# A long convolution with gating on one core: the second stage's early loads cut in halves and issued by ScalarE

## The chip, the cores and the metric

The kernel runs on 1 core of one Trainium2 chip. The metric is the device time of one execution in microseconds (us). The core has five engines that work side by side: TensorE (PE; its weight loads are PEld), VectorE (DVE), ScalarE (ACT), GpSimd (POOL) and SyncE (SP). Sixteen DMA engines move data between the chip's memory and SBUF. All data are f32.

## The reference, cut to what matters

Eight sequences of 6400 rows and 128 channels are convolved along the rows with a filter that is as long as a sequence. The result goes through a gated product: a causal convolution of five taps per channel with a sigmoid, times a projection, and a second projection.

```python
Xf = np.fft.rfft(x, n=2 * S, axis=1)          # x: 8 x 6400 x 128
Hf = np.fft.rfft(h, n=2 * S, axis=0)          # h: 6400 x 128
y = np.fft.irfft(Xf * Hf[None], n=2 * S, axis=1)[:, :S]
...
for k in range(5):
    gate_pre += conv_w[k] * yp[:, k:k + S, :] # yp: y behind four rows of zeros
gate = 1.0 / (1.0 + np.exp(-gate_pre))
out = (gate * (y @ w_val)) @ w_out
```

## The kernel before, in words

The transform of 6400 points is split into 100 x 64 and made of matmuls. A sequence passes four stages.

1. First stage (`Forward`): sums and differences of x (`sums`, on POOL) and products with the table `r1` (`half`), written to `gy`. Its input comes in 16 pieces `x_81` to `x_83`, three buffers of 256 KB; `sums` also issues the load of the piece three places ahead.
2. Second stage (`s2_mm`, `Product`): 13 blocks. Block kb multiplies `gy` with block kb of the table `m2` (512 KB), multiplies the result on DVE with block kb of the filter's spectrum (`hd` in the chip's memory, 512 KB, loaded into `h_sb`), and adds on POOL back into `gy`. `m2` has three buffers and the spectrum four; all seven are parts of one tile, `ring`. A block's buffer is loaded anew when its block is done (`m2_load(kb + M2B)`, `h_load(kb + HB)`).
3. Third stage (`s3_quads`): 16 groups over `gy`. Per group TensorE makes the products with `r3`; ScalarE copies one half of the result to a part of `ring` (`keep`, 128x512) and two edges to `dt` (`ends`); DVE joins both halves into `dt` (two joins).
4. Fourth stage (`Chunk`): 13 chunks over `dt`, with the table `m4` in `m4_sb`, then the taps, the sigmoid, both projections and the store to `out`.

The stages of neighbouring sequences are interlaced. The loop over the 16 groups `g` of the third stage of sequence b also holds one `half` and one `sums` of the first stage of sequence b + 1 and the remaining taps and projections of sequence b - 1 (`steps[g]`). The loop behind it holds the fourth stage of b and the second stage of b + 1. A "third stage" below means the first of these loops with all that is in it. In the first sequence there is no earlier one, and its loop also forms the weights `w_sb` (`wgen`) and loads pieces of `m4` (`m4_load`, of five rows of the table each) in the order of the list `m4_rest`.

The order on every engine is that of the program: `_Engines` wraps each engine so that instructions stay in the order written. The profile therefore names line 112, the wrapper's, for all of them, and groups are told apart by their tiles (`pt` is PSUM; `r_sb`, `m_sb` and `sd` are the tables and the sums). SyncE issues every DMA, also in program order: an issue whose buffer isn't free keeps the later ones waiting. Of the second stage's blocks, `m2` 0 to 2 and spectrum 0 to 2 are loaded ahead, in the third stage's loop, at the groups that the table `AHEAD` gives: `AHEAD[g] = (1, kb)` is spectrum block kb, `(0, kb)` is table block kb. Spectrum block 3 uses the buffer that `keep` writes, so it is loaded behind the last group.

Parts of `ring` also hold outputs and taps of the sequence before (`held_c`, `held_y`, `keeps`). So a load ahead has to wait until the chunk that uses its place has been stored. A landing is told by one of eight counters, which the DMAs of the program take in turn.

Of the kernel before, what the change touches and what calls it, by code (L numbers as in the profile page):

```python
# [16 lines left out]
C = 128  # L17
# [7 lines left out]
SB = 4  # L25
# [5 lines left out]
CH = 5  # L31
# [8 lines left out]
M2B = 3  # L40
MH = 6
HB = 4
XB = 3
XH = 8
AHEAD = {2: (1, 0), 7: (0, 0), 9: (0, 1), 10: (0, 2), 11: (1, 1), 13: (1, 2)}


def _out_range(ch):
# [76 lines left out]
def longconv_moe(ctx: ExitStack, tc: tile.TileContext, x, h, r1, m2, r3, m4, w64, out):  # L125
    nc = _Engines(tc)
# [24 lines left out]
    m2_sb = [r.rearrange("p (s a c) -> p s a c", a=2, c=C) for r in ring_at[:M2B]]  # L151
    h_sb = [ring_at[M2B + i] for i in (2, 0, 1, 3)]
# [9 lines left out]
    hd = dp.tile([NKB, 128, 2 * SB * C], F32, name="hd")  # L162
# [68 lines left out]
    def single():  # L231
        return ps1.tile([128, 512], F32, name="pt1", tag="pt1")
# [47 lines left out]
    def count(kb):  # L280
        return min(SB, HR - kb * SB)
# [7 lines left out]
    def m2_load(kb, ms=m2_sb):  # L289
        if kb < NKB:  # L290
            n = count(kb)
            nc.sync.dma_start(ms[kb % len(ms)][:, :n], m2[:, kb * SB : kb * SB + n])

    def h_load(kb):
        if kb < NKB:
            n = 2 * count(kb) * C
            nc.sync.dma_start(h_sb[kb % HB][:, :n], hd[kb, :, :n])

    def laid(t, kb):
        n = count(kb)  # L300
        return t[:, : 2 * n * C].rearrange("p (c d k t) -> p c d k t", c=2, k=n, t=2)
# [54 lines left out]
    def s3_quads(d0):  # L356
        pt = pair()
        for q in range(4):
            for c in range(2):
                for r, k in ((0, 0), (1, 0), (1, 1), (0, 1)):  # L360
                    d, o = k * HP + d0 + q, (r + k) % 2
                    w = d // 2 * 2 * N1 + c * 2 * HR + d % 2
                    v = pt[o * HP : (o + 1) * HP, k, q * 2 * N2 : (q + 1) * 2 * N2].rearrange("p (b m) -> p b m", b=2)
                    nc.tensor.matmul(
                        v[:, :, c::2],
                        lhsT=gyf[r * HP : (r + 1) * HP, w : w + 2 * HP - 1 : 2],
                        rhs=r3_sb[r * HP : (r + 1) * HP, c, :],
                        start=True,
                        stop=True,
                    )  # L370
        v = pt.rearrange("p k (d b m) -> p b m k d", b=2, m=N2)
        a = d0 // 4 % 2 * 512
        t = h_sb[HB - 1][:, a : a + 512]
        o = dv.rearrange("p n c (k d) -> p (n c) k d", k=2)[:, :, :, d0 : d0 + 4]

        def keep():
            act(
                t.rearrange("p (m c d) -> p m c d", c=2, d=2 * XG)[:, :, ::-1],
                pt.rearrange("p k (d b m c) -> p b m c (k d)", b=2, m=N2 // 2, c=2)[:, 1],
            )  # L380

        def join(op, n):
            u = t.rearrange("p (m k d) -> p m k d", k=2, d=XG)
            nc.vector.tensor_tensor(out=n, in0=v[:, 0, 2:], in1=u[:, 2:], op=op)

        def ends():
            act(o[:, 0:2], v[:, 0, :2])
            act(o[:, N2 : N2 + 2], v[:, 1, :2])

        return keep, ends, lambda: join(ADD, o[:, 2:N2]), lambda: join(ALU.subtract, o[:, : N2 + 1 : -1])  # L390
# [171 lines left out]
        m2_load(kb, m2_head)  # L562
    nc.sync.dma_start(r3_sb, r3)

    def m4_load(j):
        a = slice(CH * j, CH * j + CH + (j == 12))
        nc.sync.dma_start(m4_sb[:, a], m4.rearrange("k (n t) -> k n t", t=MW)[:, a])

    m4_rest = [12, 7, 5, 8, 4, 9, 10, 11, 6]
    sp, pr = {0: Spectrum(0)}, {}  # L570
    for kb in range(-1, NKB + 1):
        if 0 <= kb < NKB:
            pr[kb] = Product(kb, sp[kb].h, t_head[kb % 3], m2_head)
            m2_load(kb + MH, m2_head)
        if kb + 2 < NKB:
            sp[kb + 2] = Spectrum(kb + 2)
        if kb + 1 < NKB:
            sp[kb + 1].copy()
            sp[kb + 1].store()
        if 0 <= kb < NKB:  # L580
            pr[kb].mul_u()
            pr[kb].mul_t()
            pr[kb].add(nc.vector if kb == NKB - 1 else nc.gpsimd)
        if 0 <= kb < M4H:
            m4_load(kb)
# [10 lines left out]
    for b in range(B):  # L596
        nxt = b + 1 < B


        steps = collections.defaultdict(list)  # L600
        for c in pend:
            a = c.ch[0]
            if a == HEAD[0]:
                t = NS - 1
            elif c.held:
                t = (a - HELD) // CH
            else:
                k = (a - WAIT) // CH
                t = max(3 + k, 2 + 2 * k)
                steps[2 * k] += [lambda c=c: c.taps(range(2))]  # L610
                steps[2 * k + 1] += [lambda c=c: c.taps(range(2, 4)), c.add]
            steps[t] += [c.project, c.sigm, c.gate]
            if t + 2 < NS:
                steps[t + 2] += [c.output]
                steps[t + 3] += [c.store]
        pend = [c for c in pend if c.ch[0] in (HEAD[0], HEAD[0] - CH)]
        for g in range(NS):
            e = s3_quads(4 * g)
            f = []
            if nxt:  # L620
                f = fx.half([single(), single()])
                fx.sums(nc.gpsimd)
            for u in e:
                u()
            for u in f:
                u(act)
            if b == 0:
                next(wgen, None)
                next(wgen, None)
                if g % 3 == 0 and g < 12:  # L630
                    m4_load(m4_rest.pop(0))
            if nxt and g in AHEAD:
                f, kb = AHEAD[g]
                (h_load if f else m2_load)(kb)
            for u in steps[g]:
                u()
        if nxt:
            h_load(HB - 1)
        if b + 2 < B:
            fx = Forward(x[b + 2], gy)  # L640


        chs = CHUNKS if not nxt else sorted(CHUNKS, key=lambda c: (c != HEAD, c[0] > 0, c[0] < LATE))
        cs = [Chunk(b, i, ch, nxt) for i, ch in enumerate(chs)]
        jobs = collections.defaultdict(list)
        for i, c in enumerate(cs):
            if i and not c.late and not c.held:
                jobs[i + 3].append(c)
        if not nxt:
            jobs[NCH + 2].append(cs[0])  # L650
        pr = {}

        def s2(kb):
            if nxt and kb < NKB:
                pr[kb] = Product(kb)
                m2_load(kb + M2B)

        def times(kb):
            if kb in pr:
                pr[kb].mul_u()  # L660
                pr[kb].mul_t()
                pr.pop(kb).add()
                h_load(kb + HB)

        outs, at = [], 0
        for s in range(max(NCH, *jobs) + 2):
            kbs = list(range(at, min(at + 2 - s % 2, NKB))) if nxt else []
            at += len(kbs)
            if s == 0:
                s2(0)  # L670
            if s < 2:
                cs[s].s4()
            late = pend[s : s + 1]
            if late and s == 0:
                late[0].output()
                late[0].store(p_t[1][:, : HEAD[1]])
                late = []
            for kb in kbs[:1]:
                s2(kb + 1)
            if m4_rest:  # L680
                m4_load(m4_rest.pop(0))
            for c in jobs[s]:
                c.project()
            if 1 < s < NCH:
                cs[s].s4()
            for c in outs + late:
                c.output()
            for c in jobs[s]:
                c.sigm()
            for kb in kbs[:1]:  # L690
                times(kb)
            for kb in kbs[1:]:
                s2(kb + 1)
            if s < NCH:
                cs[s].copies()
            for c in outs + late:
                c.store()
            for kb in kbs[1:]:
                times(kb)
            if 0 < s <= NCH and not cs[s - 1].late:  # L700
                cs[s - 1].taps()
            if 2 < s < NCH + 2 and not cs[s - 2].late:
                cs[s - 2].add()
            for c in jobs[s]:
                c.gate()
            outs = jobs[s]
            if b + 2 < B:
                if s == 5:
                    fx.load(XB)
                if s in (9, 10):  # L710
                    fx.sums(nc.gpsimd)
        pend = [cs[0]] + [c for c in cs if c.held or c.late]
# [45 lines left out]
```

## Time and profile before

| | us |
|---|---|
| median of 3 runs | 983.11 |
| lowest, highest | 981.2, 993.21 |
| the profiled execution | 983.02 |
| its span in the trace | 980.9 |

The span runs from the first to the last instruction; the execution is 2.1 us longer. In the trace the eight third stages begin at about 99, 207, 319, 430, 543, 655, 765 and 877 us, and the fourth stage that follows each takes the rest to the next. Each line of a view names an engine, an operation, what it writes and reads (out<-in), the shape and how often (x); behind it stand the time, and in brackets the engine's idle time ahead of it and what ended that. "issue" as a releaser means that the profile shows nothing the engine waited for.

### The profile page before, as it was taken

To read this page: it belongs to the slowest core of one execution; us is meant where nothing else is said; L and a number is where in the kernel's file an instruction comes from. 1 tells how busy PE (TensorE), PEld (TensorE's weight loads), DVE (VectorE), ACT (ScalarE), POOL (GpSimd) and SP (SyncE) were. 2 spreads that over 40 slices of the span, in tenths; PEclk is the share of its full clock that TensorE was granted. 3 is DMA by queue.
4 is the path that set the end of the run, shared out by engine and by line. 5 is a ranking of instruction groups with operands and counts; after the bars stand their busy time and mean duration, and the time that the engine had idled before them with its cause. 6 is when DMAs were issued, how large, how long until landed. Compare 5 with 4: busy or idle time off the path is not lost.

```text
span 980.9 us, 47924 instructions
## 1 busy us (share of the span) xinstructions
PE 861.9 (88%) x21360; PEld 695.4 (71%) x21360; DVE 749.7 (76%) x1049; ACT 507.6 (52%) x1215; POOL 574.1 (59%) x594
## 2 busy tenths in 40 slices
PE   7799759988899989998899989989799988998797
PEld 6698758965688557965688557976588657874564
DVE  5547647878788788878797887878888786878686
ACT  4422443277624774177624774168624775156476
POOL 5447644866377664867367654866458664852132
PEclk9899789999999999999999999999999999999999
DMA  7776456826494465926495375834485365911112
GB/s 252 242 271 235 156 184 222 310 57 206 139 320 144 130 218 176 317 57 175 141 309 174 110 224 163 316 95 160 157 293 190 110 206 161 324 33 55 53 43 104
DMA packets 76365, 177.41 MB, mean 181 GB/s; under 512 B 17792, under 2 KB 29312, under 8 KB 76160
## 3 DMA queue, kind: packets, MB, share of 16 engines
q1 hardware_dynamic: 76160, 174.35, 53.8%
q8 instruction: 168, 2.75, 1.2%
q14 instruction: 37, 0.30, 0.1%
HBM read 141.56 MB, written 32.77 MB: 178 GB/s over the span
## 4 chain that ended last, share of the span: by engine, by line
PE 52%; DVE 13%; issue 8%; ACT 5%; DMA 4%; POOL 1%; SPq 0%; DVEq 0%; ACTq 0%; POOLq 0%
PE pt L112 52%; DVE ring L112 6%; DVE dt L112 4%; DMA ring<-m 3%; ACT ring L112 3%; DVE gl L112 2%; DVE gy L112 1%; POOL gl L112 1%; ACT gy L112 1%; ACT dt L112 1%; DMA out<-dt 0%; ACT p L112 0%; ACT yl L112 0%; POOL ring L112 0%; ACT gl L112 0%
## 5 line engine op out<-in xcount | busy, mean ns | idle before, releaser
L112 POOL TENSOR_TENSOR gy<-gy,ring 128x512 f32<-128x512 f32 (+1 forms) x182 | 220.3, 1242 | 119.0 <-ACT p L112 51.1
L112 PEld LDWEIGHTS pt<-r_sb,gy 64*64 64x64 f32 x8192 | 149.4, 140 | 107.8 <-issue 68.5
L112 DVE TENSOR_TENSOR dt<-pt,ring 128x496 f32<-128x496 f32 x256 | 160.0, 666 | 82.1 <-ACT dt L112 49.5
L112 PEld LDWEIGHTS pt<-m_sb,dt 128*64 128x64 f32 x4096 | 186.4, 136 | 30.3 <-issue 12.1
L112 POOL TENSOR_TENSOR sd<-x 128x256 f32<-128x256 f32 x236 | 185.4, 815 | 31.4 <-issue 19.7
L112 PE MATMUL pt<-r_sb,gy 64*64 64x64 f32 x8192 | 166.7, 228 | 41.6 <-issue 30.3
L112 PE MATMUL pt<-m_sb,dt 128*64 128x100 f32 x4096 | 194.4, 249 | 8.8 <-DVE ring L112 6.4
L112 PE MATMUL pt<-gy,ring 128*64 128x128 f32 x3008 | 188.2, 278 | 11.9 <-DMA ring<-m 5.2
L112 ACT COPY ring<-pt 128x512 f32<-128x512 f32 (+2 forms) x216 | 129.0, 603 | 130.8 <-PE pt L112 79.4
L112 PEld LDWEIGHTS pt<-gy,ring 128*64 128x64 f32 x3008 | 174.7, 135 | 24.5 <-PE pt L112 9.9
L112 PE MATMUL pt<-r_sb,sd 50*64 50x100 f32 x4608 | 148.0, 263 | 30.4 <-issue 20.9
L112 DVE TENSOR_TENSOR gy<-pt,ring 128x1024 f32<-128x1024 f32 (+1 forms) x99 | 117.0, 1181 | 59.3 <-PE pt L112 57.5
L112 PEld LDWEIGHTS pt<-r_sb,sd 50*64 50x64 f32 x4608 | 123.7, 144 | 37.9 <-issue 26.7
L112 DVE TENSOR_TENSOR ring<-pt,ring 128x1024 f32<-128x1024 f32 (+2 forms) x131 | 134.4, 1026 | 6.7 <-ACT ring L112 0.2
L112 ACT COPY gy<-pt 128x400 f32<-128x400 f32 x248 | 111.4, 506 | 34.2 <-PE pt L112 33.3
L112 ACT COPY yl<-pt 128x500 f32<-128x500 f32 (+1 forms) x89 | 51.1, 574 | 132.0 <-PE pt L112 125.4
L112 POOL TENSOR_TENSOR gl<-gl,p 128x500 f32<-128x500 f32 (+1 forms) x45 | 53.2, 1184 | 110.8 <-DVE gl L112 89.2
L112 ACT COPY dt<-pt 128x16 f32<-128x16 f32 (+3 forms) x317 | 67.2, 264 | 91.2 <-PE pt L112 91.0
L112 DVE SCALAR_TENSOR_TENSOR gl<-yl,w_sb,gl 128x500 f32<-128x500 f32 (+1 forms) x112 | 99.5, 893 | 2.1
L112 PE MATMUL pt<-ring,w_sb 128*64 128x500 f32 x320 | 80.1, 598 | 8.9 <-DVE ring L112 8.8
L112 DVE SCALAR_TENSOR_TENSOR ring<-pt,w_sb,ring 128x500 f32<-128x500 f32 (+3 forms) x94 | 63.1, 671 | 6.1 <-ACT ring L112 1.5
L112 POOL TENSOR_TENSOR ring<-ring,p 128x500 f32<-128x500 f32 (+1 forms) x23 | 24.7, 1074 | 60.7 <-DVE ring L112 44.1
(58 smaller groups left out, 781.0 us busy)
## 6 DMA issues: line engine op xcount, KB each, us to landing
ring<-m SPq DMA_DIRECT2D x90, 512.0 KB, 5.3
ring<-hd SPq DMA_DIRECT2D x84, 512.0 KB, 5.1
x<-xl SPq DMA_DIRECT2D x118, 256.0 KB, 3.0
out<-ring SPq DMA_DIRECT2D x40, 250.0 KB, 3.4
out<-yl SPq DMA_DIRECT2D x40, 250.0 KB, 2.8
m_sb<-m SPq DMA_DIRECT2D x12, 375.0 KB, 5.7
hd<-ring SPq DMA_DIRECT2D x8, 512.0 KB, 4.5
out<-dt SPq DMA_DIRECT2D x16, 250.0 KB, 4.4
```

What stands on the lines that cost most here:

```text
L112: return self._tc.keep_in_program_order(call(*args, **kwargs))
```

## The change

`AHEAD` has twelve entries in place of six. Each loads one half of a block (256 KB): of a spectrum block the first or second half of its columns, of a table block the first or second two of its four slices. They stand at groups 0, 1 and 6 to 15, one a group. ScalarE issues them, and the place in the loop is another: behind `keep`, `ends` and the joins of the group, ahead of the copies of the first stage, where before it was behind those copies. In the first sequence, the four `m4` pieces of the loop (at groups 0, 3, 6 and 9) become eight, of two rows and of three (or four), at groups 0 to 7.

```diff
-AHEAD = {2: (1, 0), 7: (0, 0), 9: (0, 1), 10: (0, 2), 11: (1, 1), 13: (1, 2)}
+AHEAD = {
+    0: (1, 0, 0), 1: (1, 0, 1), 6: (0, 0, 0), 7: (0, 0, 1), 8: (0, 1, 0), 9: (0, 1, 1),
+    10: (0, 2, 0), 11: (0, 2, 1), 12: (1, 1, 0), 13: (1, 1, 1), 14: (1, 2, 0), 15: (1, 2, 1),
+}
...
+    def ahead(spectrum, kb, half):
+        i = half * SB // 2
+        if spectrum:
+            k = slice(2 * C * i, 2 * C * i + SB * C)
+            nc.scalar.dma_start(h_sb[kb % HB][:, k], hd[kb, :, k])
+        else:
+            j = kb * SB + i
+            nc.scalar.dma_start(m2_sb[kb % M2B][:, i : i + SB // 2], m2[:, j : j + SB // 2])
...
-    def m4_load(j):
-        a = slice(CH * j, CH * j + CH + (j == 12))
+    def m4_load(j, half=None):
+        a = CH * j, CH * j + CH + (j == 12)
+        if half is not None:
+            a = (a[0] + 2 * half, a[1] if half else a[0] + 2)
+        a = slice(*a)
         nc.sync.dma_start(m4_sb[:, a], m4.rearrange("k (n t) -> k n t", t=MW)[:, a])
...
             for u in e:
                 u()
+            if nxt and g in AHEAD:
+                ahead(*AHEAD[g])
             for u in f:
                 u(act)
             if b == 0:
                 next(wgen, None)
                 next(wgen, None)
-                if g % 3 == 0 and g < 12:
-                    m4_load(m4_rest.pop(0))
-            if nxt and g in AHEAD:
-                f, kb = AHEAD[g]
-                (h_load if f else m2_load)(kb)
+                if g < 8:
+                    m4_load(m4_rest[0], g % 2)
+                    if g % 2:
+                        m4_rest.pop(0)
             for u in steps[g]:
                 u()
```

On SyncE, in the second sequence's third stage, groups 8 to 15 read like this before (`m` is the table `m2`, `hd` the spectrum, `xl` the input):

```order
L112 DMA x_82<-xl 128x512
L112 DMA x_83<-xl 128x512
L112 DMA ring<-m 128x1024
L112 DMA out<-yl_75 128x500
L112 DMA x_81<-xl 128x512
L112 DMA ring<-m 128x1024
L112 DMA ring<-hd 128x1024
L112 DMA out<-yl_76 128x500
L112 DMA ring<-hd 128x1024
L112 DMA out<-yl_77 128x500
L112 DMA out<-yl_78 128x500
L112 DMA ring<-hd 128x1024
```

And so in the changed kernel:

```order
L115 DMA x_82<-xl 128x512
L115 DMA x_83<-xl 128x512
L115 DMA out<-yl_75 128x500
L115 DMA x_81<-xl 128x512
L115 DMA out<-yl_76 128x500
L115 DMA out<-yl_77 128x500
L115 DMA out<-yl_78 128x500
L115 DMA ring<-hd 128x1024
```

The input loads and the stores now follow each other without a load of `ring` between them; only spectrum block 3, the last row, is left on this queue.

On ScalarE, groups 9 and 10 of the same stage read like this before; in brackets stand the counters that an instruction waits for:

```order
L112 COPY ring<-pt_3628 128x32x2x8 [waits PE_49,Activation_49]
L112 COPY dt<-pt_3628 128x4x4 x2
L112 COPY gy<-pt_3661 128x400 [waits PE_49]
L112 COPY gy<-pt_3662 128x400
L112 COPY yl_75<-pt_3616 128x500
L112 COPY ring<-pt_3694 128x32x2x8 [waits DVE_49,PE_49,Activation_49]
L112 COPY dt<-pt_3694 128x4x4 x2
L112 COPY gy<-pt_3727 128x400 [waits PE_49]
L112 COPY gy<-pt_3728 128x400
```

And so in the changed kernel:

```order
L115 COPY ring<-pt_3641 128x32x2x8 [waits PE_49,Activation_49]
L115 COPY dt<-pt_3641 128x4x4 x2
L115 DMA ring<-m 128x512 [waits DMAHW1_49]
L115 COPY gy<-pt_3674 128x400 [waits PE_49]
L115 COPY gy<-pt_3675 128x400
L115 COPY yl_75<-pt_3629 128x500
L115 COPY ring<-pt_3707 128x32x2x8 [waits DVE_49,PE_49,Activation_49]
L115 COPY dt<-pt_3707 128x4x4 x2
L115 DMA ring<-m 128x512 [waits DMAHW4_49,DMAHW3_49]
L115 COPY gy<-pt_3740 128x400 [waits PE_49]
L115 COPY gy<-pt_3741 128x400
```

A half now stands between the third stage's copies and the first stage's, and waits for one of the eight landing counters, the one that it takes itself, and at the second of the two also for an earlier store from its place in `ring`.

At the start of that stage, groups 0 and 1, ScalarE's row was before:

```order
L112 COPY dt<-pt_2982 128x4x4 [waits DMAHW4_49]
L112 COPY dt<-pt_2982 128x4x4
L112 COPY gy<-pt_3015 128x400 [waits PE_49]
L112 COPY gy<-pt_3016 128x400
L112 ACTIVATE ring<-ring 128x500 [waits Pool_49]
```

And it is now:

```order
L115 COPY dt<-pt_2992 128x4x4 [waits DMAHW6_49]
L115 COPY dt<-pt_2992 128x4x4
L115 DMA ring<-hd 128x512 [waits Pool_49]
L115 COPY gy<-pt_3025 128x400 [waits PE_49]
L115 COPY gy<-pt_3026 128x400
L115 ACTIVATE ring<-ring 128x500 [waits DVE_49]
```

The first half of spectrum block 0 waits there for POOL, which reads its place in the last step of the stage before.

## The prediction

> **What bounds the kernel now.** I read the page first, for shares. TensorE is busy 88% of the span, and the chain that ended last lies on it for half. The chain also has 8% of "issue", time in which an engine waited for nothing that the profile shows.
>
> ```profile
> PE 861.9 (88%) x21360; PEld 695.4 (71%) x21360; DVE 749.7 (76%) x1049; ACT 507.6 (52%) x1215; POOL 574.1 (59%) x594
> q8 instruction: 168, 2.75, 1.2%
> PE 52%; DVE 13%; issue 8%; ACT 5%; DMA 4%; POOL 1%; SPq 0%; DVEq 0%; ACTq 0%; POOLq 0%
> ```
>
> The waits say whose issue time it is:
>
> ```profile
> PEld pt L112 <- issue: 139.7, 220, 3.3
> PE pt L112 <- issue: 53.1, 39, 3.1
> ```
>
> Then the table by stage (columns: stretch; length; busy time of PE, PEld, DVE, ACT, POOL with counts; clock; DMA share; GB/s). A third stage (99 to 152 in the first sequence, 207 to 263 in the second) has 1,574 matmuls and as many weight loads; the stage behind it has 996 in the same 56 us.
>
> ```profile
> 99.00:152.00 53.00, 37.24 (x1527) 35.44 (x1531) 29.69 (x53) 23.85 (x76) 24.53 (x33) 0.81 0.50 158
> 207.00:263.00 56.00, 47.57 (x1574) 31.45 (x1578) 42.41 (x64) 40.68 (x109) 32.82 (x38) 1.00 0.50 157
> 263.00:319.00 56.00, 52.89 (x996) 48.14 (x988) 46.30 (x58) 19.59 (x39) 38.63 (x37) 1.00 0.64 216
> ```
>
> The page's q8 moved 168 packets for 42,720 TensorE instructions, one for 254: I read it as TensorE's program arriving by DMA. The timeline of the weight loads bears that out; they stop in the middle of a run of equal instructions, in the first sequence for 3.24 us:
>
> ```profile
> 136.38 0.29 PEld L112 LDWEIGHTS pt<-r_sb,sd 50*64 50x64 f32 x5 [0.55 <-issue]
> 138.39 0.54 PEld L112 LDWEIGHTS pt<-r_sb,gy 64*64 64x64 f32 x24
> 142.16 0.64 PEld L112 LDWEIGHTS pt<-r_sb,gy 64*64 64x64 f32 x36 [3.24 <-issue]
> 146.34 0.21 PEld L112 LDWEIGHTS pt<-r_sb,gy 64*64 64x64 f32 x8 [1.95 <-issue]
> 150.07 0.34 PEld L112 LDWEIGHTS pt<-r_sb,sd 50*64 50x64 f32 x8 [0.28 <-issue]
> ```
>
> TensorE resumes at 136.38 and stops again after the run that begins at 138.39. SyncE had queued 512 KB loads just before; in 136.4 to 139.8 the 16 DMA engines carry data alone, and the instruction packet is in the next stretch, 139.8 to 142.2:
>
> ```profile
> 135.24 0.44 SPq L112 DMA_DIRECT2D ring<-m  x1
> 135.72 0.91 SPq L112 DMA_DIRECT2D ring<-hd  x2
> ...
> DMA packets 380, 1.20 MB, mean 354 GB/s; under 512 B 39, under 2 KB 39, under 8 KB 380
> q1 hardware_dynamic: 380, 1.20, 100.5%
> ...
> q8 instruction: 1, 0.02, 2.4%
> ```
>
> After 146.34 no data moves. 146.4 to 147.7 is empty, and 147.7 to 150 holds the packet alone:
>
> ```profile
> DMA packets 0, 0.00 MB, mean 0 GB/s; under 512 B 0, under 2 KB 0, under 8 KB 0
> ...
> q8 instruction: 1, 0.02, 2.5%
> ```
>
> So from resuming to the packet it is about 3.4 us behind data and 1.4 us without, and one block of program takes 5.78 us (136.38 to 142.16) against 3.73. This bounds the first sequence's third stage, and in the later ones the "issue" on the chain. Of those six stages' chains, the second sequence's and the sixth's:
>
> ```profile
> by line: PE pt L112 59.9%; issue 16.3%; DVE ring L112 6.5%; ACT ring L112 5.7%; DVE dt L112 4.5%; DVE gl L112 2.2%; ACT gy L112 1.5%; POOL gl L112 1.5%; ACT p L112 1.1%; POOL ring L112 0.5%; ACT dt L112 0.3%; POOLq L112 0.1%; DVEq L112 0.1%
> by line: PE pt L112 86.0%; issue 12.8%; DVE ring L112 1.3%
> ```
>
> That is 9.1 us of 56 and 6.9 us of 54.
>
> **The change part by part.** *Halves, one per group.* The same bytes are loaded, so only queueing can fall. At 354 GB/s a 512 KB load holds the engines 1.48 us, a half 0.74, an x load of 256 KB 0.74, a store of 250 KB 0.72. The second stretch's 3,152 instructions are 12.4 packets in 56 us, or 0.22 per us. A packet that arrives at random behind a run of transfers of length L waits L/2, so a run costs 0.22 x L²/2. Now a load often stands in a pile with an x load and a store: in 458.5 to 462.4 the data were 1.02 MB, and the chain then shows 2.08 us of issue.
>
> ```profile
> DMA packets 425, 1.02 MB, mean 261 GB/s; under 512 B 54, under 2 KB 169, under 8 KB 425
> ...
> 462.74 2.08 issue
> 464.82 1.19 PE pt L112 x24
> ```
>
> Piled, L is 2.94 us. Six piles and six groups with x and store apart (0.53 each) make L²/2 = 25.9 + 3.2 = 29.1; twelve halves each apart from x and store make 12 x (0.27 + 0.53) = 9.7. The difference is 19.4 x 0.22 = 4.3 us per sequence. If the halves pile up too (L = 2.2), it is 12 x 2.42 = 29.0: nothing gained. I take 2.0, a little under half: ScalarE sends a half behind its copies of the group, the x load goes when POOL has freed its buffer, but some of the loads stand nearly alone now. Seven sequences give 14 us (bounds 0 and 30). On the path: PE and issue are 76% and 99% of the two chains above; the first third of the others runs by DVE. With 0.75 it is **-10.5 us** (0 to -22).
>
> *Moved to ScalarE.* Twelve issues in seven sequences, 84. SyncE's take 0.33 to 0.44 us:
>
> ```profile
> 443.15 0.33 SPq L112 DMA_DIRECT2D x<-xl  x1
> 443.53 0.42 SPq L112 DMA_DIRECT2D ring<-hd  x1
> ...
> 431.41 0.59 ACT L112 COPY ring<-pt 128x512 f32<-128x512 f32 x1 [0.56 <-PE pt L112]
> 431.90 0.25 ACT L112 COPY dt<-pt 128x16 f32<-128x16 f32 x2
> 432.10 0.89 ACT L112 COPY gy<-pt 128x400 f32<-128x400 f32 x2
> ```
>
> No row shows a ScalarE issue. If it stopped the engine it would cost 84 x 0.33 = 28 us; if its queue prepares it under the copies ahead, nothing. The copies from 431.41 overlap their successors (0.59 us long, 0.49 to the next), so work is queued ahead there, and ScalarE is busy 40.7 of 56 us. I take **+2** (0 to 28). Behind the issue stand the two gy copies, and TensorE for their banks. [...]
>
> The issue also waits: for POOL's last additions at groups 0 and 1, and for landing counters, taken in turn by all DMAs, so for the transfer eight places earlier. That is two to three groups, over 7 us, against a median landing of 5.3 us or less: nothing, and if that cover went, 1 us each would stop ScalarE.
>
> ```profile
> ring<-m SPq DMA_DIRECT2D x90, 512.0 KB, 5.3
> ring<-hd SPq DMA_DIRECT2D x84, 512.0 KB, 5.1
> x<-xl SPq DMA_DIRECT2D x118, 256.0 KB, 3.0
> ```
>
> *First half at group 0* (now at group 2, 443.53). It comes 2 us behind the last store of dt, whose landing lets the first join on DVE start:
>
> ```profile
> 430.04 0.55 SPq L112 DMA_DIRECT2D out<-dt  x1
> 434.25 1.25 DVE L112 TENSOR_TENSOR dt<-pt,ring 128x496 f32<-128x496 f32 x2 [4.66 <-PE pt L112]
> ```
>
> The row names TensorE, which had released ScalarE's copy at 431.41 already; the store is later. Sharing costs 0 to 0.74 us at six boundaries; I take 0.35, **+2** (0 to 4.4).
>
> *Last half at group 15.* It now goes at about 375 in the third sequence. The product that needs it starts 9 us later, more than the 5.1 us landing above: 0.
>
> ```profile
> 375.25 1.25 DVE L112 TENSOR_TENSOR dt<-pt,ring 128x496 f32<-128x496 f32 x2 [1.17 <-ACT dt L112]
> 384.49 1.22 DVE L112 TENSOR_TENSOR gy<-pt,ring 128x1024 f32<-128x1024 f32 x1
> ```
>
> *SyncE* sheds 42 issues and gets four more for the table's pieces, 38 x 0.33 = 13 us of a queue that mostly waits: 0. The pieces' halves end at group 7 (before: group 9); their saving is in the 2.0.
>
> Sum: -10.5 + 2 + 2 = **-6.5 us**. The profiled execution took 983.0 us (span 980.9), 0.1 below the median of 983.1, so 976.5. Afterwards the DVE chain in each stage's first third is what is late next.
>
> **The rivals.** *Nothing changes (983).* The bytes are the same, and a packet may wait for its own engine's backlog whichever pieces it is cut in. For it: the stages' DMA share stays 0.50. Against: 3.4 us against 1.4 above. [...]
>
> *The piles vanish (955 to 963).* The whole 4.3 us per sequence, on the path throughout, is 30 us: 953; with the costs 957. Against it: DVE is busy 42.4 of 56 us and takes over.
>
> *ScalarE pays (1002; slower).* Each issue stops ScalarE for 0.33 us: +28 in place of +2, with the gain of 10.5 and the dt store 983 - 10.5 + 28 + 2 = 1002.5. It turns slower than before from 8.5 / 84 = 0.10 us per issue on the path. For it: half of the halves go where ScalarE is TensorE's only relief for banks. Against: its idle quarter.
>
> **How the numbers follow.** Mine 0.50 (966 to 982), nothing 0.27 (981 to 986), piles vanish 0.12, ScalarE pays 0.11. Predicted 976.5. The range 962 to 988 leaves out 0.10 below and 0.09 above. A measurement of this kernel tells about 2% (20 us) from no change, so faster is below 963.4, slower above 1002.8: 0.12, 0.82 and 0.06; half of "ScalarE pays" reaches slower.
>
> **What would show it.** Right: "PEld <- issue" falls from 139.7 us by some 15, the third stages (207 to 263) last about 1 us less, and the first sequence's some 2 us less; the stage behind keeps 56 us. ScalarE's rows show gy copies at the same distance from the keep copy; if they move out by 0.3 us, it pays. The first join's wait grows by up to 0.7 us. Wrong: "issue" unchanged at shorter transfers, or ScalarE waiting for DMA.

## The result and the profile after

| | before | after |
|---|---|---|
| median of 4 runs, us | 985.52 | 970.43 |
| lowest, highest, us | 981.2, 993.21 | 967.63, 972.54 |
| the profiled execution, us | 983.02 | 968.37 |
| its span, us | 980.9 | 966.3 |

The ratio is 0.9855 with a 95% interval of 0.9815 to 0.9894: 14.3 us less on 985.5, inside the 2% that a measurement of this kernel tells from no change, yet clearly below 1. A fourth run of the kernel before, made with these, moved its median from 983.1 to 985.5. Below, a ratio is turned into microseconds by (ratio - 1) x 985.5.

The page of the changed kernel, with its share of the span by engine, its DMA queues and the last chain:

```profile
span 966.3 us, 48005 instructions
PE 855.1 (88%) x21360; PEld 687.5 (71%) x21360; DVE 748.4 (77%) x1049; ACT 506.4 (52%) x1215; POOL 575.5 (60%) x594
q1 hardware_dynamic: 70688, 152.33, 47.7%
q10 hardware_dynamic: 12096, 22.03, 8.2%
q8 instruction: 168, 2.75, 1.2%
PE 54%; DVE 19%; issue 11%; DMA 7%; ACT 5%; POOL 3%; SPq 1%; DVEq 0%; ACTq 0%; POOLq 0%
ring<-hd ACTq DMA_DIRECT2D x42, 256.0 KB, 3.4
ring<-m ACTq DMA_DIRECT2D x42, 256.0 KB, 4.0
x<-xl SPq DMA_DIRECT2D x118, 256.0 KB, 3.5
```

The 84 halves (84 x 256 KB = 22.0 MB) are a queue of their own, q10, which is ScalarE's. They land 3.4 and 4.0 us after their issue; the loads of x take 3.5 where they took 3.0. The shares of the two last chains can't be set side by side as they stand: the chain before starts at 153 us, this one at 1.6. Over the stretch that both cover, from the end of the first third stage on, issue is 9.8% before and 10.0% after, and DVE's four largest lines (`ring`, `dt`, `gl`, `gy`) are 15.4% and 21.7%.

The waits of the changed kernel (who waited for whom: us in total, times, longest):

```profile
PEld pt L115 <- issue: 130.3, 223, 2.5
PE pt L115 <- issue: 45.2, 38, 2.3
PEld pt L115 <- ACT gy L115: 14.3, 27, 1.2
```

TensorE waits 9.4 us less for its program ahead of weight loads and 7.9 us less ahead of matmuls, and the longest such wait is 2.5 us in place of 3.3.

On balance the gain lies in the third stages. The table by stage (the first and second third stage and the stage behind the second, columns as in the prediction):

```profile
97.00:148.00 51.00, 33.38 (x1536) 31.65 (x1536) 29.10 (x55) 24.00 (x76) 25.14 (x34) 0.90 0.54 159
202.00:257.00 55.00, 48.41 (x1616) 32.53 (x1614) 43.63 (x64) 40.11 (x109) 33.84 (x39) 1.00 0.55 155
257.00:314.00 57.00, 52.69 (x984) 47.95 (x980) 47.02 (x59) 20.12 (x41) 38.87 (x37) 1.00 0.65 217
```

The stretches are cut by hand. The length is told better by the first and the last of the 1,024 matmuls of a third stage, in the view of one tile (shortest, median, longest in ns; starts of the first and the last). Before, first and second sequence:

```profile
L112 PE MATMUL pt<-r_sb,gy x1024: 217/221/366, 99.1 to 151.6; 64*64 64x64 f32 x171
L112 PE MATMUL pt<-r_sb,gy x1024: 212/220/272, 206.9 to 263.1; 64*64 64x64 f32 x171
```

After:

```profile
L115 PE MATMUL pt<-r_sb,gy x1024: 217/220/363, 97.9 to 147.3; 64*64 64x64 f32 x171
L115 PE MATMUL pt<-r_sb,gy x1024: 212/220/272, 202.8 to 256.7; 64*64 64x64 f32 x171
```

The first two third stages went from 52.5 to 49.4 us and from 56.2 to 53.9. By the same rows of the seven sequences with loads ahead, the third stages sum to 385.4 us before and 370.6 after. These 14.8 us are as much as the whole difference of the two profiled executions (14.65); what else moved cancels out (the stages between them are 2.7 us longer in all, the work ahead of the first and behind the last some 3 us shorter).

In the second to the seventh third stage it is the gaps that shrank: by the table by stage, cut at these matmuls, TensorE stands idle there 35.3 us in all, where it was 45.3, and is busy 287.2 us, where it was 288.9. The first is another case. Its rows have TensorE busy 33.38 us at a granted clock of 0.90, where it was 37.24 at 0.81, with almost the same median matmul (221 and 220 ns); its idle time did not shrink (51.00 - 33.38 = 17.6 us, where it was 15.8). Over the whole run TensorE is busy 855.1 us where it was 861.9, for the same 21,360 matmuls. What got shorter in the first stage is the time to the next piece of program. By the start times of q8's packets in both traces, TensorE restarts there 2.2 to 2.9 us after a packet has started; from a restart to the start of the next packet, the nine blocks that can be compared took 19.6 us before and 15.8 after. By these rows 3.9 us less of busy time goes with 1.8 us more of idle time; that the matmuls, once faster, only wait longer for the next piece of program is a reading of these numbers. Why the granted clock differs, and whether it has a part in that time, is not shown.

The first sequence's weight loads show what became of the 3.24 us stop. The timeline of the changed kernel, the same place (the longest stop in the first third stage, and the last three):

```profile
126.03 1.03 PEld L115 LDWEIGHTS pt<-r_sb,gy 64*64 64x64 f32 x58
129.52 0.20 PEld L115 LDWEIGHTS pt<-r_sb,gy 64*64 64x64 f32 x4 [2.46 <-issue]
...
137.56 0.63 PEld L115 LDWEIGHTS pt<-r_sb,gy 64*64 64x64 f32 x36 [1.62 <-issue]
...
141.74 0.21 PEld L115 LDWEIGHTS pt<-r_sb,gy 64*64 64x64 f32 x8 [1.95 <-issue]
...
146.03 0.23 PEld L115 LDWEIGHTS pt<-r_sb,sd 50*64 50x64 f32 x8 [0.83 <-issue]
```

The stops are still there, one per block of program, but none of them is over 2.5 us.

### The profile page after: what moved, and what is told of

Read it like the earlier page. It is cut to its first block, busy times and chain, and to the rows that moved or that the text cites. A ratio compares the mean times of both kernels' runs of the same rounds, so it can differ in the third digit from the quotient of the medians.

```text
span 966.3 us, 48005 instructions
## 1 busy us (share of the span) xinstructions
PE 855.1 (88%) x21360; PEld 687.5 (71%) x21360; DVE 748.4 (77%) x1049; ACT 506.4 (52%) x1215; POOL 575.5 (60%) x594
## 4 chain that ended last, share of the span: by engine, by line
PE 54%; DVE 19%; issue 11%; DMA 7%; ACT 5%; POOL 3%; SPq 1%; DVEq 0%; ACTq 0%; POOLq 0%
PE pt L115 54%; DVE ring L115 7%; DVE dt L115 5%; DMA ring<-m 4%; DVE gl L115 4%; ACT ring L115 3%; DVE gy L115 2%; POOL gl L115 2%; ACT gl L115 1%; DMA ring<-hd 1%; ACT dt L115 1%; DMA x<-xl 1%; POOL sd L115 1%; SPq L115 1%; POOL gy L115 1%
## 5 line engine op out<-in xcount | busy, mean ns | idle before, releaser
L115 PEld LDWEIGHTS pt<-r_sb,gy 64*64 64x64 f32 x8192 | 144.4, 137 | 103.5 <-issue 62.2
L115 PEld LDWEIGHTS pt<-m_sb,dt 128*64 128x64 f32 x4096 | 184.9, 136 | 30.3 <-issue 12.5
L115 PE MATMUL pt<-r_sb,gy 64*64 64x64 f32 x8192 | 162.0, 225 | 36.9 <-issue 24.0
L115 PEld LDWEIGHTS pt<-gy,ring 128*64 128x64 f32 x3008 | 174.6, 135 | 24.5 <-PE pt L115 10.1
L115 PE MATMUL pt<-r_sb,sd 50*64 50x100 f32 x4608 | 144.7, 261 | 26.4 <-issue 19.9
L115 PEld LDWEIGHTS pt<-r_sb,sd 50*64 50x64 f32 x4608 | 121.3, 143 | 33.0 <-issue 22.2
```

The source lines that it names most:

```text
L115: return self._tc.keep_in_program_order(call(*args, **kwargs))
```

## The experiments

After the result, two theories could make the gain: that the loads are in halves and spread over the groups ("halves"), or that another engine issues them ("issuer"). Each experiment was compared with the kernel before in the same rounds. Executions of one kernel differ by up to some 10 us (those of the kernel with ScalarE as the only change lie between 969.7 and 979.0), so single profiles serve below for a mechanism, and ratios for a size.

**The halves, issued by SyncE again.**

```diff
-            nc.scalar.dma_start(h_sb[kb % HB][:, k], hd[kb, :, k])
+            nc.sync.dma_start(h_sb[kb % HB][:, k], hd[kb, :, k])
...
-            nc.scalar.dma_start(m2_sb[kb % M2B][:, i : i + SB // 2], m2[:, j : j + SB // 2])
+            nc.sync.dma_start(m2_sb[kb % M2B][:, i : i + SB // 2], m2[:, j : j + SB // 2])
```

> The changed kernel with one thing undone: SyncE issues the halves, at the same groups and the same place in the loop. Theory (queueing): TensorE's instruction packets wait behind shorter and more evenly spread loads, whoever issues them; then the gain stays, 0.983 to 0.990 of the kernel before. Rival (issuer): the gain comes from taking loads off SyncE's queue, where they stand among input loads and stores; then it goes, 0.997 to 1.003. In between means that both count.

979.58 us, ratio 0.993 (0.9901 to 0.9959): -6.9 us, about half of the gain. Halves and places alone don't make it; the other half goes with ScalarE. On SyncE the halves can go in the same moment as the loads of x, as its timeline in this kernel shows:

```profile
457.77 0.33 SPq L115 DMA_DIRECT2D x<-xl  x1
458.20 0.37 SPq L115 DMA_DIRECT2D ring<-m  x1
```

**Whole blocks from ScalarE, at the new groups.**

```diff
-AHEAD = {
-    0: (1, 0, 0), 1: (1, 0, 1), 6: (0, 0, 0), 7: (0, 0, 1), 8: (0, 1, 0), 9: (0, 1, 1),
-    10: (0, 2, 0), 11: (0, 2, 1), 12: (1, 1, 0), 13: (1, 1, 1), 14: (1, 2, 0), 15: (1, 2, 1),
-}
+AHEAD = {0: (1, 0), 6: (0, 0), 8: (0, 1), 10: (0, 2), 12: (1, 1), 14: (1, 2)}
...
+            nc.scalar.dma_start(h_sb[kb % HB], hd[kb])
...
+            nc.scalar.dma_start(m2_sb[kb % M2B], m2[:, kb * SB : kb * SB + SB])
```

> The changed kernel with whole blocks of 512 KB, issued by ScalarE at groups 0, 6, 8, 10, 12 and 14, the groups of the first halves. Queueing: the piles are back, half or more of the gain goes, 0.990 to 1.000. Issuer: nothing is lost, 0.983 to 0.988.

976.04 us, ratio 0.9898 (0.9865 to 0.9931): -10.1 us. By the ratios, most of the gain is there without cutting these loads (the table's pieces are still in halves).

**No load ahead at all in the third stages.**

```diff
+AHEAD = {}
```

> The changed kernel without any load ahead in the third stages: blocks 0 to 2 of the table and of the spectrum are not loaded there, so the second stage works on what lies in the buffers. Queueing: what is left of the packets' wait behind these loads goes too, so each of the first seven third stages becomes 1 to 2 us shorter than in the changed kernel, 0.970 to 0.980 of before. Rival (the loads no longer matter after the change): 0.983 to 0.988.

965.94 us, ratio 0.9801 (0.9766 to 0.9836): -19.6 us. The first two third stages and TensorE's waits in this kernel's trace, by the views used above:

```profile
L112 PE MATMUL pt<-r_sb,gy x1024: 217/220/366, 97.5 to 145.8; 64*64 64x64 f32 x171
L112 PE MATMUL pt<-r_sb,gy x1024: 213/220/272, 201.4 to 253.9; 64*64 64x64 f32 x171
```

```profile
PEld pt L112 <- issue: 119.3, 216, 2.8
PE pt L112 <- issue: 32.4, 32, 2.7
```

With 22 MB less to load, TensorE waits 20 us less for its program ahead of weight loads than before. So the loads ahead do hold the program up, and all that this lever could bring on balance is some 20 us; the change has 14 of them. The third stages alone are 26 us shorter than before in this trace (359.0 us in all), and the stages between them 8 us longer.

**The table's pieces whole again, the rest as changed.**

```diff
-                if g < 8:
-                    m4_load(m4_rest[0], g % 2)
-                    if g % 2:
-                        m4_rest.pop(0)
+                if g % 3 == 0 and g < 12:
+                    m4_load(m4_rest.pop(0))
```

> The changed kernel with the last table's four pieces of the first sequence whole again, at groups 0, 3, 6 and 9. The first third stage became 3.2 us shorter by the trace (52.5 to 49.3). Queueing: the pieces are half of the bytes cut there, so 1 to 2 us of it come back and nothing else moves, 0.985 to 0.989. Rival (they matter nothing): 0.983 to 0.987, and the first third stage stays at 49 us.

973.36 us, ratio 0.9883 (0.9845 to 0.9921): 2.8 us worse than the changed kernel, which the intervals don't resolve. In its profile the first third stage, the only one with these loads, is as long as after (49.4 us). What halving the table's pieces brings stays open between 0 and some 3 us. One profile of that stage tells little in any case: it is 49.0 us long too in the kernel with SyncE's load ahead of x below, where nothing is halved and nothing was gained.

**Whole blocks from ScalarE, at the old groups.** As the second experiment, with the numbers of before:

```diff
+AHEAD = {2: (1, 0), 7: (0, 0), 9: (0, 1), 10: (0, 2), 11: (1, 1), 13: (1, 2)}
```

> Whole blocks at the groups of before (2, 7, 9, 10, 11, 13), issued by ScalarE behind the group's keep and edge copies; the last table's pieces in halves as in the changed kernel. Only the issuer of the second stage's loads and the halved last table differ from before. Queueing: 0.993 to 1.000, the first sequence's 1 to 2 us and no more. Issuer: 0.983 to 0.988.

973.38 us, ratio 0.9866 (0.983 to 0.9901). This is close to the changed kernel's ratio (0.9855), without its halves of blocks and its new groups.

**Both halves of a block together, at the six groups.**

```diff
+AHEAD = {0: (1, 0), 6: (0, 0), 8: (0, 1), 10: (0, 2), 12: (1, 1), 14: (1, 2)}
...
-                ahead(*AHEAD[g])
+                ahead(*AHEAD[g], 0)
+                ahead(*AHEAD[g], 1)
```

> Halves, but both of a block one behind the other at the groups 0, 6, 8, 10, 12 and 14, issued by ScalarE. If spreading is what counts, it is like whole blocks at these groups. If the size of one transfer is what counts, it is like the changed kernel, 0.983 to 0.988.

973.51 us, ratio 0.988 (0.9838 to 0.9921). It lies between whole blocks at these groups (0.9898) and spread halves (0.9855), and is resolved from neither.

**The first block's halves at groups 2 and 3 in place of 0 and 1.**

```diff
-    0: (1, 0, 0), 1: (1, 0, 1), 6: (0, 0, 0), 7: (0, 0, 1), 8: (0, 1, 0), 9: (0, 1, 1),
+    2: (1, 0, 0), 3: (1, 0, 1), 6: (0, 0, 0), 7: (0, 0, 1), 8: (0, 1, 0), 9: (0, 1, 1),
```

> The changed kernel with the spectrum's block 0 at groups 2 and 3 in place of 0 and 1. In the changed kernel the first join of DVE starts 4.4 to 5.5 us behind the issue of the last store of dt, before 4.1 to 4.6; the mean is 0.50 us more at six boundaries. If the half at group 0 causes that, the wait goes back to 4.1 to 4.6 us and 2 to 3 us are gained, 0.981 to 0.984. Rival (DVE makes it up, or groups 2 and 3 are as bad): 0.984 to 0.988.

970.47 us, ratio 0.9836 (0.9803 to 0.9868): 1.9 us better than the changed kernel by the ratios, not resolved. From the issue of the last store of `dt` to the first join it is a mean of 4.74 us at the six boundaries, against 4.83 after and 4.33 before: three boundaries go back to 4.2 to 4.4, three do not.

**Each half loaded twice.**

```diff
                 ahead(*AHEAD[g])
+                ahead(*AHEAD[g])
```

> The changed kernel with each half loaded twice, one load behind the other from ScalarE: 21 MB more, the same result. Queueing: L goes from 0.74 to 1.48 us for twelve runs per sequence, 0.22 x 12 x (1.10 - 0.27) = 2.2 us per sequence alone and up to three times that in piles, so 15 to 40 us more than the changed kernel, 1.000 to 1.025 of before. Rival (data don't delay the packets): 0.983 to 0.990.

1121.06 us, ratio 1.1382 (1.1346 to 1.1419). This was a miss as a test of queueing. The second load writes where the first does, and so waits for its landing, on ScalarE, with the copies behind it. The waits of this kernel:

```profile
ACT gy L115 <- DMA ring<-m: 101.9, 40, 4.9
ACT gy L115 <- DMA ring<-hd: 85.1, 36, 4.8
PEld pt L115 <- ACT gy L115: 139.8, 61, 6.3
```

ScalarE's copies stand 187 us behind landings, and TensorE 139.8 us behind ScalarE where it was 14.3. What it does tell is the price of an issue that waits there: (1121.1 - 970.4) / 84 = 1.8 us each.

**The kernel before, with ScalarE as the issuer and nothing else.** ScalarE sends the six whole loads at the old groups, ahead of its `gy` copies; the table's pieces stay whole on SyncE.

```diff
+            if nxt and g in AHEAD:
+                ahead(*AHEAD[g])
             for u in f:
                 u(act)
...
-            if nxt and g in AHEAD:
-                f, kb = AHEAD[g]
-                (h_load if f else m2_load)(kb)
```

> The kernel before with one thing changed: ScalarE issues the six whole loads ahead, at the same groups, behind the group's keep and edge copies. Nothing is halved, the last table's pieces neither. Theory now (issuer): this alone brings most of the change, 0.985 to 0.991. Rival (halves): 0.996 to 1.001, and what the kernel with old groups gained was the halved last table.

974.94 us, ratio 0.9896 (0.9851 to 0.994): -10.2 us. Changing the issuer, and with it the place inside the group, brings by the medians more than halves spread over the groups on SyncE (-6.9); the two are not resolved from each other.

Its trace shows less than its ratio. The profiled execution, the slowest of its six (979.01 us), has a span only 3.7 us below that of before, and TensorE's wait for its program is almost the same (139.7 before):

```profile
PEld pt L112 <- issue: 136.3, 221, 4.0
```

**The kernel before, with SyncE's load ahead of the group's load of x.**

```diff
             e = s3_quads(4 * g)
+            if nxt and g in AHEAD:
+                w, kb = AHEAD[g]
+                (h_load if w else m2_load)(kb)
```

> The kernel before with one thing changed: in its group, SyncE's load ahead stands in front of the group's input load, not behind it, so that it doesn't go out in one burst with an input load that had waited for POOL. Theory (apart): what counts is that the loads leave apart from the input loads, whichever queue they are on; a good part of the gain comes, 0.988 to 0.995. Rival (second queue): what counts is that these loads are on a queue of their own, 0.997 to 1.003.

989.27 us, ratio 1.0011 (0.9977 to 1.0045): nothing, 11.3 us above the kernel of the last experiment, with intervals that don't overlap. The earlier place in the group is therefore not what the issuer's kernel gains by. But it did not part the load from its neighbours either. SyncE's rows in this kernel:

```profile
459.55 0.33 SPq L112 DMA_DIRECT2D x<-xl  x1
459.97 0.38 SPq L112 DMA_DIRECT2D ring<-m  x1
```

SyncE's row is empty for 3.2 us ahead of these two (its issue before them ends at 456.36), and then sends them 0.42 us apart: read as one instruction that waits, and what has gathered behind it. With ScalarE as issuer (the experiment before) the same loads go at moments that SyncE's row doesn't set; some still fall close to a load of x, as the first one here. SyncE's loads of x, then ScalarE's rows:

```profile
453.62 0.33 SPq L112 DMA_DIRECT2D x<-xl  x1
455.52 0.42 SPq L112 DMA_DIRECT2D x<-xl  x1
460.57 2.14 SPq L112 DMA_DIRECT2D x<-xl  x2
```

```profile
455.06 0.36 ACTq L112 DMA_DIRECT2D ring<-m  x1
461.67 0.34 ACTq L112 DMA_DIRECT2D ring<-m  x1
463.31 0.33 ACTq L112 DMA_DIRECT2D ring<-m  x1
```

Over the third stages, the median distance from a load ahead to the nearest other issue, worked out from such rows, is 0.42 us before, 0.43 with halves on SyncE and 0.39 here; it is 1.26 us in the issuer's kernel, 0.88 with whole blocks at the new groups, and 0.69 after. With whole blocks from ScalarE at the old groups it is 1.48, and with both halves together 0.37, each half being the other's neighbour.

**Spare copies behind each half.** 84 more transfers of 256 KB, from one place of the chip's memory to another, issued by ScalarE.

```diff
                 ahead(*AHEAD[g])
+                nc.scalar.dma_start(spare[next(spares)], m2[:, : SB // 2])
```

> The changed kernel with 84 copies of 256 KB within the chip's memory, that nothing needs, one behind each half, issued by ScalarE. It mends the doubled loads, where the second had to wait for the first on the same place. Queueing: TensorE's packets wait longer, 0.22 x 12 x (1.10 - 0.27) = 2.2 us a sequence alone and up to three times that in piles: 10 to 40 us over the changed kernel, 0.995 to 1.025 of before, and the PEld waits for issue rise from 130 us by 10 or more. Rival (data don't delay the packets): 0.983 to 0.990, and these waits stay.

994.0 us, ratio 1.0096 (1.0064 to 1.0128): 24 us above the changed kernel. Its waits:

```profile
PEld pt L115 <- issue: 139.5, 227, 3.0
PEld pt L115 <- ACT gy L115: 26.8, 31, 2.6
```

TensorE waits 9.2 us longer for its program ahead of weight loads, so more data holds it up more. But it also waits 12.5 us longer for ScalarE, which some of the spare issues stopped: the one at 467.86 lasts 2.08 us, and the next `gy` copy starts at 469.98, as it ends. The direction is confirmed; the size is not queueing alone.

**More loads moved.** The changed kernel with the first block at groups 2 and 3, and the ten later table blocks of the second stage issued by ScalarE too.

```diff
+    def m2_scalar(kb):
+        if kb < NKB:
+            n = count(kb)
+            nc.scalar.dma_start(m2_sb[kb % M2B][:, :n], m2[:, kb * SB : kb * SB + n])
...
-                m2_load(kb + M2B)
+                free.append(kb + M2B)
...
+            if s < NCH and free:
+                m2_scalar(free.pop(0))
```

> The kernel with the spectrum's block 0 at groups 2 and 3 (e7), and besides the ten later blocks of the table in the second stage issued by ScalarE, behind its copies of the step, where SyncE had them behind spectrum loads that wait for POOL. Theory (issuer): a load that leaves SyncE's row goes when its own buffer is free; in the trace of the changed kernel the matmuls wait 6.2 us for these loads, and the chain has about 7 us of them in each such stage, so 3 to 8 us less than e7, 0.976 to 0.981 of before. Rival (ScalarE stops for these waits, or the row was no limit there): 0.983 to 0.995.

965.63 us, ratio 0.9821 (0.9778 to 0.9863), the lowest median of all, and not resolved from the same kernel without it (0.9836). Its waits show why more loads on ScalarE bring little:

```profile
PE pt L115 <- DMA ring<-m: 5.0, 4, 1.5
DVE gy L115 <- DMA ring<-hd: 14.2, 9, 2.8
```

TensorE waits for the table as long as in the kernel that this one is built on (5.0 us; 6.2 after), and DVE's product now waits 14.2 us for the spectrum, which SyncE still loads.

## Why the prediction was right in sign and half the size

The time of 970.43 lies in the range and on the side that were forecast, and TensorE's wait for its program fell as forecast. But the sum was -6.5 us, and -14.3 came. That it lies in the range is in part luck: the halves alone, on SyncE, gave -6.9, and the move, counted as a cost of 0 to 28 us, gained some 10 alone by its ratio. By the terms:

**"Halves, one per group", -10.5.** Here the reason was right, and the share of the cut is not settled. That loads hold up TensorE's program is borne out from both sides: without the loads ahead the wait falls by 20 us, with more data it grows by 9. The reading of 3.4 us against 1.4 holds too: from the restarts at 136.38 and 146.34 to the starts of the next packets it is 3.5 and 1.4 us. But the whole gain was given to the cut. By the ratios, given ScalarE as issuer, cutting and spreading bring some 4 us at most, and are not resolved: 0.9898 with whole blocks at the new groups, 0.9866 at the old, 0.9855 after. On SyncE they bring 6.9. The traces divide it otherwise. In the second to the seventh third stage TensorE stands idle 45.3 us before and 43.7 with SyncE's load ahead of x; 40.4 to 42.8 in the three kernels with whole blocks from ScalarE; 40.2 with halves from SyncE; and 32.8 to 38.0 in the five with halves from ScalarE and nothing loaded twice or copied besides. There the cut brings more than the issuer does. The three profiled executions with whole blocks are each the slowest of their six, so the traces don't overrule the ratios; in both, the lowest value belongs to a kernel with halves from ScalarE. What the piles of the prediction owe to SyncE's row, which sends a load together with whatever else had gathered behind a wait (0.4 us apart), was not asked.

**"Moved to ScalarE", +2.** This is the step that failed. It was priced only as a cost, of its 84 issues, and no cost shows. ScalarE's rows of the changed kernel at the first join of the fourth sequence:

```profile
425.13 0.58 ACT L115 COPY ring<-pt 128x512 f32<-128x512 f32 x1 [0.56 <-PE pt L115]
425.14 0.33 ACTq L115 DMA_DIRECT2D ring<-hd  x1
425.61 0.26 ACT L115 COPY dt<-pt 128x16 f32<-128x16 f32 x2
425.82 0.89 ACT L115 COPY gy<-pt 128x400 f32<-128x400 f32 x2
```

The issue runs from 425.14 to 425.47, inside the copy ahead of it, and the `gy` copies start 0.69 us after the keep copy, as in the quoted rows of before (431.41 to 432.10). Over all groups of the seven third stages the median of this distance is 0.65 us before and after. By its ratio the move was worth -10.2 us instead, alone; its trace, as said, shows only a part of that. The prediction did write down that ScalarE sends a half behind its copies while x goes when POOL has freed a buffer, and used that only to choose within the halves' 4.3 us, from which it took "a little under half"; as a term of the move it needs no halves.

**"First half at group 0", +2.** The wait grew by the size taken; its cause is not shown. The first join starts 4.83 us after the last store of `dt` is issued, against 4.33 before: 0.50 at six boundaries, 3.0 us, where 0.35 was taken. SyncE's and DVE's rows of the changed kernel:

```profile
423.73 0.55 SPq L115 DMA_DIRECT2D out<-dt  x1
```

```profile
428.15 1.26 DVE L115 TENSOR_TENSOR dt<-pt,ring 128x496 f32<-128x496 f32 x2 [4.85 <-DMA ring<-hd]
```

The row names the half because its landing is the last by the profile; that is inferred. And the mean is 4.74 us with this half moved to group 2, and 4.40 with halves at the same groups but on SyncE. Moving it later is worth 1.9 us by the medians of ratios, which no run resolves, so the term is neither confirmed nor refuted.

**"Last half at group 15" and "SyncE", 0.** Nothing speaks against either. The stages between the third ones are 0.4 us longer on the mean (2.7 us over seven, from the last of the quoted matmuls to the first of the next stage), which is within what executions of one kernel differ by.

**What would show it.** "PEld <- issue" was to fall by some 15 us and fell by 9.4, with 7.9 more ahead of matmuls. The third stages were to be 1 us shorter and the first one 2; they are 0.9 to 3.6 shorter, the first one 3.1. In the first one, the sum of these waits did not fall (16.4 us before, 17.3 after, ahead of weight loads), since TensorE's busy time fell by more than the stage did. The forecast that DVE is late next fits the chains, 21.7% in place of 15.4% over the stretch that both cover.

**The rivals.** "Nothing changes" fell: with the same bytes to load, TensorE's wait for its program ahead of weight loads went from 139.7 to 130.3 us. That wait also moves with the bytes: it is 119.3 us without the 22 MB of loads ahead and 139.5 with 22 MB more. "The piles vanish" was too much: even with no load left, 19.6 us is the gain, not 30. "ScalarE pays" fell, but its mechanism is real where the issue has to wait: 1.8 us each with every half loaded twice.

**What stays open.** How much of the gain is the issuer's, and why it helps. Two readings fit: the loads no longer go in one burst with SyncE's, or they are a second queue (q10) beside q1 and so hold the instruction packets less. The kernel made to tell them apart, SyncE's load ahead of that of x, did not part the loads. Bursts follow the times in some runs, but halves on SyncE gain 6.9 us at unchanged bursts (0.43 us apart), and whole blocks 1.48 us apart are no faster than halves 0.69 apart. A third possibility, that the granted clock and not the loads makes a part of the difference, is not excluded: its mean over the runs is 0.976 before, 0.981 with the issuer alone and 0.985 after. Whether fewer stops keep the clock up or the clock came first, no run tells. Loads parted on one queue, or in a burst on two, were not tried.

## What to carry to other kernels

Before cutting a large load, ask also who issues it: look at the issuing queue's row for transfers that go out 0.4 us apart behind one wait. By its ratio, moving loads to an engine whose copies come at times of their own was worth 1% here without any cut, and its issues cost that engine nothing that could be seen so long as they need not wait; with a wait behind every issue it cost 1.8 us each. A run without the loads at all gives the bound of such a change first, here 20 us. And a stage that got shorter needs its busy time and granted clock read beside its gaps, before the gain is given to one cause.

## What the runs showed of the hardware

- TensorE's program keeps arriving by DMA all through the run (read from 168 packets on q8 before, after and in eleven of the experiments), and its wait for it moves with the data around it: 119.3 us ahead of weight loads with none of the loads ahead, 130.3 after, 139.5 after with 22 MB of spare copies.
- In the first third stage TensorE restarts 2.2 to 2.9 us after an instruction packet has started, in both traces; from a restart to the start of the next packet it takes 1.4 to 3.5 us before and 1.4 to 2.4 us after, over the nine blocks compared.
- ScalarE's DMA issue takes 0.33 us beside its copies, without moving them: the median distance from keep copy to `gy` copy is 0.65 us before and after. When it waits for a landing, its copies wait too (187 us in all with each half loaded twice).
- The same halves land in 3.4 us (spectrum) and 4.0 us (table) from ScalarE's queue. The first experiment's kernel sends them from SyncE, and its DMA issues show 4.0 for both (with 15 other loads of that size among them):

```profile
ring<-m SPq DMA_DIRECT2D x50, 256.0 KB, 4.0
ring<-hd SPq DMA_DIRECT2D x49, 256.0 KB, 4.0
```
